# A matmul-bound retention, MLP and mixture-attention kernel: own PSUM banks for turned tiles, seven products for one more block, new ranks

## The chip, the cores and the metric

The kernel runs on one core of a Trainium2 chip. The metric is the device time of one launch in microseconds (us). The kernel before takes 442.72 us, the median of three runs (442.19 to 445.38). Lower is better.

## The reference

Three stages follow each other on 2 sequences of 768 tokens, all in float32.

```python
# 1. retention, 8 heads of 64, per head:  state = gamma*state + k_t v_t^T ;  y_t = q_t state / 8
# 2. MLP on x (768 x 512):
xn = (x - mu) / np.sqrt(var + 1e-06) * g_ln
ch = np.maximum(xn @ w_ch1, 0.0) @ w_ch2          # 512 -> 2048 -> 512
x = x + ch
# 3. mixture of 4 attention experts of width 64, the best 2 per token:
logits = x @ w_gate                                # top 2 of 4, softmax of the two -> w
q, k, v = x @ wq[e], x @ wk[e], x @ wv[e]
a = softmax(causal(q @ k.T / 8)); ye = a @ v @ wo[e]
out = sum over the two chosen experts of w * ye
```

## The kernel before, in words

**Front.** Retention is done in chunks of 128 tokens: 12 chunks (6 for each sequence b), each by `r_tile`. A chunk loads `kq` (512 KB) and `vk` (512 KB; 256 KB in each sequence's last chunk). TensorE computes scores (line 581), the part that comes from the state (600), the part inside the chunk (610) and the new state (618). VectorE scales into `xT`; TensorE turns that tile (`turn`, line 422) into PSUM, VectorE takes mean and variance from there (642), GpSimd the root (650), ScalarE normalises out of PSUM (`xn`, 655), TensorE turns it back (422) and ScalarE copies it to `xc` (664). The two turned tiles of a chunk are of kind `pb`. In the kernel before, a `pb` or `pc` tile is half of two PSUM banks, at the same columns of both (1024 words hold two such tiles), so two turned tiles share a pair of banks.

**MLP.** The 2048 hidden columns are worked in 8 blocks `f` of 256. Each float32 number is split into a rounded high part and the rest (`h`, `l`), and each product is three matmuls (high x high, high x low, low x high). Blocks 0 and 1 take plain products (`m_h`, line 766, then `m_c`, line 788). In blocks 2 to 7 (`SEVEN`) the first product, over both halves of the 768 tokens at once, goes by `m_h7` (line 858): seven half-sized products and sums of them (Strassen's scheme in Winograd's form) in place of eight. It needs sums of the weights (`w_sums`, GpSimd, in blocks 2 and 3 VectorE too) and of the tokens (`x_sums`). The second product, `m_c`, is plain in all blocks. The weights come as 64-bit floats and are cut down to 32 bits by ScalarE, GpSimd and VectorE (`split_piece`, lines 685 to 719).

**Attention.** `q_proj` (952) and `q_val` (976) make q, k and v of one sequence. `a_scores` works a strip of 128 queries against the keys before it for two experts: TensorE (1047), VectorE adds the mask and takes the row maximum (1054), ScalarE the exponential (1062), VectorE the inverse sum (1068, 1069), GpSimd scales the strip (1076). `a_turn` turns pieces of four 128-wide slots through PSUM (`pc` tiles, line 422) and ScalarE or VectorE copies each out (`COPY`, 446). `a_value` (1117) multiplies by v, `a_out` (1144) by `wo`, and the rows leave by DMA. The strips of two query chunks, for a pair of experts, are turned and multiplied together: 12 such groups in all.

**What sets the order.** Nothing is issued in the order of the code. Every step is a `Node` with a cost for each engine that may run it, and `Plan.issue` is a list scheduler: on each engine the ready step of lowest `prio` goes next, where `prio` is the place in the code plus a number from the table `RANK`, if its tiles find free places in SBUF and PSUM (`PL` lists the places of each kind). The instructions are then recorded in that order, and each engine's queue runs strictly in it. TensorE steps have a form (`whole`, `rows`, `columns`, `quarters`: the piece of the array that a matmul uses), and the planner charges `SWITCH` for each change of form. `spin` steps are idle matmuls at the start, before data arrive.

```python
    PL["pb"] = [("P", 1024 * i + 256 * k, 256) for i in (1, 2, 3) for k in range(2)]
    PL["pc"] = [("P", 1024 * i + 256 * k, 256) for i in (3, 2) for k in range(2)]
...
    def DMA(nbytes, fn, r=(), w=()):
        P.add({"D": nbytes / 372e3 + 0.03}, lambda e: fn(), r, w, lat=2.2)
```

Of the kernel before, what the change touches and what calls it, by code (L numbers as in the profile page):

```python
# [19 lines left out]
try:  # L20
# [27 lines left out]
ALONE = 4  # L48
SWITCH = 0.125
LAST = 10000  # L50
FILL = 12
TWO = ("pb", "pc")
# [6 lines left out]
WORDS = 205 * KB  # L59
QUEUES = {"ps1": "s", "ps2": "s", "pr": "pr", "pt": "pt", "ptn": "pt", "sm": "sm", "at": "at", "w": "w", "h": "h", "raw": "raw", "wy": "wy",  # L60
          "w1": "w1", "S": "S", "t": "t", "u": "u", "sf": "sf",
          "am": "am", "vs": "vs", "xn": "xn", "xc": "xc"}
ROUNDED = {"x", "w", "w1", "S", "t", "h", "wq", "wk", "wv", "wo", "qk0", "qk1", "at"}


class Buf:
# [1249 lines left out]
```

## Time and profile before

| | |
|---|---|
| median of 3 runs | 442.72 us (442.19 to 445.38) |
| the profiled execution | 442.45 us, its span 440.7 us, so 1.75 us lie around the span |
| TensorE (PE) busy | 429.4 us, 97% of the span |
| PE weight loads | 402.4 us, beside the matmuls |
| VectorE (DVE), ScalarE (ACT), GpSimd (POOL) busy | 309.8, 217.7, 212.0 us |
| chain that ended last | PE 90%, ACT 3%, DVE 2%, DMA 2%, POOL 1% |
| mean granted TensorE clock | 0.999 of full speed |

How to read it: an engine's queue runs in order, so a wait of one instruction holds all behind it. PE's busy time is not PE at its peak, since matmuls overlap; what a step takes of PE is the time from its start to the start of the next one. The chain of waits goes back from the last instruction, and here it stays on PE for nine tenths of the span.

### The profile page before, as it was taken

The page shows a single profiled execution, that of the slowest core. Times are in us where ns is not written, and L with a number is a line of the kernel's source. Part 1 is how long each engine was busy: PE and PEld are TensorE (multiplying, and loading weights), DVE is VectorE, ACT ScalarE, POOL GpSimd, SP SyncE. Part 2 cuts the span into 40 slices and gives each one's busy share as a digit, 9 for nine tenths or more (in the row PEclk, how much of TensorE's full clock was granted, in tenths as well). Part 3 has the DMA queues.
Part 4 walks back from the last instruction along what each step waited for, and adds up shares of the span by engine and source line. Part 5 has one row for each costly group of instructions (what it writes and reads, how often), then busy time and mean ns, then how long its engine had stood idle before and what let it go on. Part 6 is the DMA issues. An engine that isn't in the chain of part 4 may idle for free.

```text
span 440.7 us, 9076 instructions
## 1 busy us (share of the span) xinstructions
PE 429.4 (97%) x3546; PEld 402.4 (91%) x3546; DVE 309.8 (70%) x743; ACT 217.7 (49%) x460; POOL 212.0 (48%) x219
## 2 busy tenths in 40 slices
PE   9988999999999999999999999999999999999996
PEld 8877889999999999999999999999999877887765
DVE  2769978765778876868877655668556778667663
ACT  1568775342656346335353264234533666656552
POOL 2668865999999528117136054200401343422430
PEclk9999999999999999999999999999999999999999
DMA  8999432210322304104112002001100001001121
GB/s 288 328 337 345 133 109 84 97 49 1 106 86 92 101 0 143 50 1 136 54 59 88 1 1 96 1 0 55 48 1 1 1 12 39 2 0 49 50 97 49
DMA packets 11995, 35.18 MB, mean 80 GB/s; under 512 B 1840, under 2 KB 2480, under 8 KB 11952
## 3 DMA queue, kind: packets, MB, share of 16 engines
q1 hardware_dynamic: 11952, 34.60, 22.7%
q8 instruction: 28, 0.46, 0.4%
q14 instruction: 15, 0.12, 0.1%
HBM read 31.45 MB, written 3.15 MB: 79 GB/s over the span
## 4 chain that ended last, share of the span: by engine, by line
PE 90%; ACT 3%; DVE 2%; DMA 2%; POOL 1%; issue 1%; SPq 0%; POOLq 0%; DVEq 0%
PE ps L788 30%; PE ps L858 20%; PE ps L766 8%; PE ps L952 8%; PE ps L1117 4%; PE ps L976 4%; PE ps L422 4%; PE ps L1144 4%; PE ps L1047 3%; DMA raw<-in_w_dram 2%; PE ps L529 2%; PE ps L610 1%; PE ps L581 1%; ACT xn L655 1%; PE ps L600 1%
## 5 line engine op out<-in xcount | busy, mean ns | idle before, releaser
L788 PE MATMUL ps<-h,w 128*128 128x384 f32 x768 | 142.4, 335 | 0.0
L788 PEld LDWEIGHTS ps<-h,w 128*128 128x128 f32 x768 | 133.7, 188 | 0.7 <-DVE ps L798 0.3
L794 DVE TENSOR_TENSOR xT<-xT,ps 128x384 f32<-128x384 f32 x112 | 60.2, 550 | 30.6 <-PE ps L788 30.1
L1076 POOL TENSOR_SCALAR pr<-pr,sm,gate 128x384 f32<-128x384 f32 (+5 forms) x48 | 34.0, 718 | 77.9 <-DVE sm L1069 34.1
L719 POOL TENSOR_TENSOR w<-wy,w 128x512 fp32r<-128x512 f32 x26 | 34.0, 1319 | 38.1 <-PE ps L788 23.4
L858 PE MATMUL ps<-t,S 128*128 128x384 f32 x216 | 42.1, 334 | 0.0
L858 PEld LDWEIGHTS ps<-t,S 128*128 128x128 f32 x216 | 37.8, 188 | 0.0
L1062 ACT ACTIVATE pr<-pr,sm 128x384 f32<-128x384 f32 (+5 forms) x48 | 31.7, 663 | 9.9 <-DVE sm L1054 9.9
L766 PE MATMUL ps<-x,w 128*128 128x384 f32 x192 | 35.2, 337 | 0.0
L877 ACT ACTIVATE h<-ps 128x384 fp32r<-128x384 f32 x36 | 17.7, 490 | 32.9 <-PE ps L788 20.6
L766 PEld LDWEIGHTS ps<-x,w 128*128 128x128 f32 x192 | 33.2, 188 | 0.3
L685 ACT ACTIVATE wx<-raw 128x512 f32<-128x512 f32 x32 | 21.5, 671 | 23.8 <-DVE ps L692 16.0
L687 POOL TENSOR_SCALAR wx<-wx 128x512 f32<-128x512 f32 x32 | 20.0, 625 | 23.9 <-ACT wx L685 23.0
L867 ACT ACTIVATE u<-ps 128x384 f32<-128x384 f32 x36 | 17.5, 488 | 25.3 <-PE ps L858 16.6
L858 PE MATMUL ps<-x,w 128*128 128x384 f32 x144 | 28.6, 334 | 0.0
L689 DVE TENSOR_SCALAR ps<-wx 128x512 uint32<-128x512 uint32 x32 | 22.0, 688 | 6.4 <-POOL wx L687 6.1
L858 PEld LDWEIGHTS ps<-x,w 128*128 128x128 f32 x144 | 25.3, 188 | 0.0
L1054 DVE CUSTOM_DVE_ANT_0 pr<-ps,mask 128x384 f32<-128x384 f32 (+4 forms) x48 | 22.1, 495 | 3.2 <-PE ps L1047 2.2
L695 DVE SCALAR_TENSOR_TENSOR wy<-raw,ps 128x512 uint32<-128x512 uint32 x32 | 21.8, 683 | 2.3 <-POOL w L719 1.7
L879 DVE SCALAR_TENSOR_TENSOR h<-ps,h 128x384 fp32r<-128x384 f32 x36 | 19.4, 551 | 5.3 <-ACT h L877 5.2
L692 DVE SCALAR_TENSOR_TENSOR ps<-wx,ps 128x512 uint32<-128x512 uint32 x32 | 22.2, 695 | 1.1
L587 DVE TENSOR_TENSOR am<-ps,caus 128x512 f32<-128x512 f32 x24 | 15.5, 683 | 9.9 <-PE ps L581 9.9
(122 smaller groups left out, 822.7 us busy)
## 6 DMA issues: line engine op xcount, KB each, us to landing
raw<-in_w_dram SPq DMA_DIRECT2D x32, 512.0 KB, 3.4
kq<-in_kq_dram SPq DMA_DIRECT2D x11, 512.0 KB, 5.1
vk<-in_vk_dram SPq DMA_DIRECT2D x9, 512.0 KB, 5.5
out_dram<-ob SPq DMA_DIRECT2D x11, 256.0 KB, 2.0
vk<-in_vk_dram SPq DMA_DIRECT2D x4, 256.0 KB, 3.8
vraw<-in_wv_dram SPq DMA_DIRECT2D x1, 520.0 KB, 3.9
kq<-in_kq_dram SPq DMA_DIRECT2D x2, 256.0 KB, 5.2
mraw<-in_wk_dram SPq DMA_DIRECT2D x1, 512.0 KB, 4.6
```

What stands on the lines that cost most here:

```text
L689: DVE(0.69, lambda: dve.tensor_scalar(u32(z), u32(x), 4, 1, op0=OP.logical_shift_left, op1=OP.logical_shift_right), r=[x], w=[z])
L692: DVE(0.7, lambda: dve.scalar_tensor_tensor(u32(z), u32(x), 0x80000000, u32(z), op0=OP.bitwise_and, op1=OP.bitwise_or), r=[x, z], w=[z])
L695: DVE(0.7, lambda: dve.scalar_tensor_tensor(u32(y), words(0), 29, u32(z), op0=OP.logical_shift_right, op1=OP.bitwise_or), r=[raw, z], w=[y])
L719: POOL(1.3, lambda: pool.tensor_tensor(f32r(l), f32(y), f32(h), OP.subtract), r=[y, h], w=[l])
L766: pe.matmul(f32(pa, TB), lhsT=wt, rhs=blk(f32r(xt[b][j]))[:, k], start=(n == 0), stop=(n == 11))
L788: pe.matmul(f32(pa, TB), lhsT=wt, rhs=t, start=(n == 0), stop=(n == 5))
L794: DVE(0.55, lambda: dve.tensor_tensor(blk(f32(xt))[:, k], blk(f32(xt))[:, k], f32(pa, TB), OP.add), r=[pa] + [(xt, cc, w) for cc in range( ...
L858: pe.matmul(f32(pa, TB), lhsT=wt, rhs=t, start=(first and n == 0), stop=(n == 5), skip_group_check=True)
L952: pe.matmul(f32(pa, TB), lhsT=mw(n, lo, k, p * 128, (p + 1) * 128), rhs=blk(f32r(xt))[:, k], start=(i == 0), stop=(i == 11))
L1054: DVE(0.22 + wide * 1.04e-3, lambda ks=ks, n=n, z=z, SC=SC: dve.tensor_tensor_reduce(f32(PR[z])[:, ks], f32(SC[z])[:, :wide], f32(MASK)[:, ...
L1062: ACT(act_c(nk) + .18, lambda pr=pr, z=z: act.activation(f32(pr, nk), f32(pr, nk), AF.Exp, bias=f32(sm)[:, z:z + 1], scale=-1.0, accum_out ...
L1076: POOL(0.34 + nk * 0.84e-3, lambda pr=pr, z=z, e=e: pool.tensor_scalar(f32(pr, nk), f32(pr, nk), f32(sm)[:, 6 + z:7 + z], GT[b, j][:, cc, ...
```

## The change

- A turned tile (`pb`, `pc`) gets two whole PSUM banks of its own; `pb` has three places in place of six, `pc` four in place of four halves. Scores (`ps1`) and attention outputs (`psa`) may lie in all eight banks. `a_turn` cuts its slots into two equal pieces rather than pieces of four (40 pieces in place of 48).
- In the last block, f = 7 (`BOTH`), the second product goes by seven products too: `m_c7`, seven products of three matmuls for each half r of the output columns, with sums of the hidden values (`ht`, made by GpSimd) and of the second weights (`S2`). `leave` is the old end of `m_c`.
- The quarter sum `c22` of `m_h7` stays in PSUM rather than in SBUF.
- `kq` and `vk` get more places (6 and 4 for 4 and 3), as do other tiles; `WORDS` grows, and the DMA scratch area is set to 1024.
- The planner's costs change: a DMA at 335 KB/us in place of 372, lead times of the engines (`LEAD`), `w_sums` on GpSimd alone. The state is one key in place of two. All of `RANK` is new, so the order is new on every engine.

```diff
@@ -46,21 +46,22 @@
+BOTH = (7,)
 SWITCH = 0.125
+LEAD = {"V": 0.085, "A": 0.1, "G": 0.05}
...
 RANK = {
-    "a_out 1": (16, (46, 145, 47, 97, -108, 150, -14, -17)),
+    "a_out 1": (16, (-6, 10, -14, 15, 85, 136, -22, 123)),
...
-        n.eng = eng
+        n.eng = {e: c - LEAD.get(e, 0.0) for e, c in eng.items()}
         n.fn = fn
-        n.lat = lat
+        n.lat = lat + max(LEAD.get(e, 0.0) for e in eng)
...
+    PL["kq"] += region(o_z, 4 * KB, 2)
+    PL["vk"] += region(o_z + 8 * KB, 4 * KB, 1)
...
-    PL["psa"] = banks[4:][::-1]
-    PL["ps1"] = banks[:4]
+    PL["psa"] = banks[::-1]
+    PL["ps1"] = banks
     PL["state"] = banks[:1]
 
-    PL["pb"] = [("P", 1024 * i + 256 * k, 256) for i in (1, 2, 3) for k in range(2)]
-    PL["pc"] = [("P", 1024 * i + 256 * k, 256) for i in (3, 2) for k in range(2)]
-
-    def two(b):
-        i, k = divmod(b.at[1], 1024)
-        return ps[:, 1024 * i:1024 * i + 1024].rearrange("p (h c) -> p h c", h=2)[:, :, k:k + 256]
+    PL["pb"] = [("P", 1024 * i, 1024) for i in (1, 2, 3)]
+    PL["pc"] = [("P", 1024 * i, 1024) for i in (3, 2, 1, 0)]
+
+    def two(b, n=256):
+        return view(b).rearrange("p (h c) -> p h c", h=2)[:, :, :n]
...
     def DMA(nbytes, fn, r=(), w=()):
-        P.add({"D": nbytes / 372e3 + 0.03}, lambda e: fn(), r, w, lat=2.2)
+        P.add({"D": nbytes / 335e3 + 0.03}, lambda e: fn(), r, w, lat=2.2)
...
         W[f, i] = (h, l)
+        if f in BOTH and i >= 2:
+            W[f, i + 2] = y
+            if i == 3:
+                w_sums(f, W[f, 4], y, True)
...
+        def out(src, n):
+            h = l = None
+            if f in BOTH:
+                t = HT[n]
+                P.at = "m_h7 4"
+                ACT(0.49, lambda: act.activation(plain(t), f32(src, TB), AF.Relu), r=[src], w=[t])
+                if n == 2:
+                    return
+                h, l = new("h"), new("h")
+                P.at = "m_h7 5"
+                ACT(0.42, lambda: act.activation(f32r(h, TB), plain(t), AF.Copy), r=[t], w=[h])
...
-        c22 = new("u")
+        c22 = new("ps")
         add(c22, pc, u3)
...
+        if f in BOTH:
+            ht = [new("ht") for _ in range(4)]
+            for t, p, q in ((0, 2, 0), (2, 1, 2), (1, 1, 0), (3, 3, 1)):
+                P.at = "m_h7 8"
+                POOL(0.93, lambda t=t, p=p, q=q: pool.tensor_tensor(plain(HT[t]), plain(HT[p]), plain(HT[q]), OP.subtract),
+                     r=[HT[p], HT[q]], w=[HT[t]])
+            for t in range(4):
+                P.at = "m_h7 9"
+                ACT(0.42, lambda t=t: act.activation(f32r(ht[t]), plain(HT[t]), AF.Copy), r=[HT[t]], w=[ht[t]])
+                P.at = "m_h7 10"
+                POOL(0.93, lambda t=t: pool.tensor_tensor(f32r(HT[t]), plain(HT[t]), f32(ht[t]), OP.subtract), r=[HT[t], ht[t]], w=[HT[t]])
+            return m_c7(f, b, {"x00": h00, "x10": h10, "x11": h11, **{f"t{t}": (ht[t], HT[t]) for t in range(4)}})
         return [h00, h10], [h01, h11]
+
+    def m_c7(f, b, tokens):
+        def second(r):
+            pa, pb, pc = (new("ps") for _ in range(3))
...
+                def mm():
+                    for i, (wt, t) in enumerate(((wh, xh), (wh, xl), (wl, xh))):
+                        pe.matmul(f32(pa, TB), lhsT=f32r(wt)[:, cs], rhs=f32r(t, TB), start=(first and i == 0), stop=(i == 2),
+                                  skip_group_check=True)
...
+            product(pa, "a0", "x00", True)
+            c1 = keep(pa)
+            yield
+            product(pb, "s1", "t1", True)
+            add(pb, pb, c1)
+            yield
+            product(pa, "y0", "x10", False)
+            leave(pa, b, 0, r)
...
-            dve.tensor_scalar(m[:, 4:6], m[:, 2:4], 1e-9, None, op0=OP.add)
+            for z in range(2):
+                dve.tensor_scalar(m[:, 4 + z:5 + z], m[:, 2 + z:3 + z], 1e-9, None, op0=OP.add)
...
-            for s0 in range(0, len(slots), 4):
-                part = slots[s0:s0 + 4]
+            half = (len(slots) + 1) // 2 if len(slots) > 4 else len(slots)
+            for s0 in range(0, len(slots), half):
+                part = slots[s0:s0 + half]
```

Three places of the new order follow, each before and after. In names like `kq_90` the number tells tiles of one kind apart; it differs between the two kernels.

TensorE at the very start of the program; `negs` rows are the idle matmuls, `kq` rows the scores of a chunk. Before:

```order
L529 MATMUL ps<-negs 128x128 x14
L581 MATMUL ps<-kq_90 128x128 x8
L581 MATMUL ps<-kq_85 128x128 x8
L529 MATMUL ps<-negs 128x128 x2
L610 MATMUL ps<-am_124,vs_109 64x128 x4
L610 MATMUL ps<-am_128,vs_109 64x128 x4
```

After:

```order
L546 MATMUL ps<-negs 128x128 x10
L598 MATMUL ps<-kq_83 128x128 x8
L546 MATMUL ps<-negs 128x128 x3
L627 MATMUL ps<-am_111,vs_107 64x128 x4
L627 MATMUL ps<-am_116,vs_107 64x128 x4
L546 MATMUL ps<-negs 128x128
```

The first chunk's scores stand behind 10 idle matmuls rather than 14, one chunk's scores go first rather than two, and four of the idle matmuls moved behind them (six in all there, for two).

SyncE's queue of loads, in the middle of the front; `raw` rows are pieces of MLP weights, `kq` and `vk` the chunks' data. Before:

```order
L505 DMA vk_322<-in_vk_dram 128x1024
L495 DMA kq_361<-in_kq_dram 128x1024
L678 DMA raw_377<-in_w_dram 128x1024
L505 DMA vk_404<-in_vk_dram 128x1024
L678 DMA raw_444<-in_w_dram 128x1024
L495 DMA kq_469<-in_kq_dram 128x1024
```

After:

```order
L522 DMA vk_443<-in_vk_dram 128x1024
L522 DMA vk_470<-in_vk_dram 128x1024
L512 DMA kq_504<-in_kq_dram 128x1024
L695 DMA raw_532<-in_w_dram 128x1024
L695 DMA raw_558<-in_w_dram 128x1024
L512 DMA kq_595<-in_kq_dram 128x1024
```

The first piece of weights is the 27th load of the queue rather than the 22nd, and the second stands right behind it: more of the chunks' data go ahead of the weights.

TensorE in the last MLP block. Before, the last rows of its plain second product, with scores of the attention already between them:

```order
L788 MATMUL ps<-h_3483,w_3049 128x384
L788 MATMUL ps<-h_3487,w_3051 128x384
L788 MATMUL ps<-h_3497,w_3051 128x384
L788 MATMUL ps<-h_3487,w_3067 128x384
L1047 MATMUL ps<-qk_531_3896,qk_547_4030 128x384 x2
L1047 MATMUL ps<-qk_531_3896,qk_548_4048 128x384 x2
```

After, where the first product with a sum of hidden values begins (`ht` and `S`; sequence b = 0); the `L811` rows ahead of it are the plain second product of block 6:

```order
L811 MATMUL ps<-h_3184,w_2757 128x384
L811 MATMUL ps<-h_3194,w_2757 128x384
L811 MATMUL ps<-h_3184,w_2771 128x384
L978 MATMUL ps<-ht_3340,S_426_2989 128x384
L978 MATMUL ps<-ht_3353,S_426_2989 128x384
L978 MATMUL ps<-ht_3340,S_428_3000 128x384
```

The last block's second product is now 84 matmuls (`L978`) in place of 96, spread among the rest of block 6, the first product of b = 1 and the first projections. 44 matmuls of other steps stand between the last matmul of `m_h7` of b = 0 and the first `ht` row, and 39 for b = 1. The first scores of the attention stand at row 1,693 of PE's order, where they stood at row 1,577.

## Rows read from the trace of the kernel before

**Rows 1.** Busy time by stage (windows): us, PE, PEld, DVE, ACT, POOL.

```profile
12.00:50.50 38.50, 34.60 (x691) 29.58 (x689) 30.66 (x75) 26.48 (x57) 28.49 (x38) 1.00 0.86 305
82.70:319.00 236.30, 236.30 (x1363) 235.87 (x1362) 169.67 (x305) 105.76 (x200) 124.00 (x101) 1.00 0.17 57
319.00:437.00 118.00, 115.21 (x1113) 96.66 (x1112) 79.18 (x301) 63.22 (x166) 33.99 (x48) 1.00 0.07 25
```

**Rows 2.** Who PE waited for: us in total, times, longest.

```profile
PE ps L422 <- DVE pt L446: 1.6, 3, 0.7
PE ps L422 <- ACT xn L655: 1.2, 1, 1.2
...
PE ps L422 <- ACT ptn L446: 0.7, 2, 0.4
```

**Rows 3.** PE in the MLP, in order of time: start, us, what.

```profile
82.70 8.49 PE L788 MATMUL ps<-h,w 128*128 128x384 f32 x48
91.03 8.48 PE L766 MATMUL ps<-x,w 128*128 128x384 f32 x48
```

**Rows 4.** PE where the form changes, in order of time.

```profile
24.08 0.41 PE L422 MATMUL ps<-ident,xn 64*128 64x64 f32 x8
24.33 0.42 PE L422 MATMUL ps<-ident,xT 64*128 64x64 f32 x8
24.68 0.67 PE L600 MATMUL ps<-kq,sn 64*64 64x128 f32 x16
...
50.50 2.38 PE L766 MATMUL ps<-x,w 128*128 128x384 f32 x12
52.81 0.46 PE L422 MATMUL ps<-ident,xn 64*128 64x64 f32 x8
53.20 2.37 PE L766 MATMUL ps<-x,w 128*128 128x384 f32 x12
```

**Rows 5.** PE at the start, in order of time.

```profile
1.05 6.00 PE L529 MATMUL ps<-negs 128*128 128x128 f32 x28 [1.05 <-DVE half L546]
6.98 2.08 PE L581 MATMUL ps<-kq 64*128 64x128 f32 x32
```

**Rows 6.** ACT in the front and PE behind it, in order of time, all engines.

```profile
28.10 0.67 ACT L685 ACTIVATE wx<-raw 128x512 f32<-128x512 f32 x1 [1.10 <-DMA raw<-in_w_dram]
...
28.94 0.77 ACT L655 ACTIVATE xn<-ps,mv 128x512 f32<-128x512 f32 x1
...
29.76 0.46 PE L422 MATMUL ps<-ident,xT 64*128 64x64 f32 x8 [1.20 <-ACT xn L655]
```

**Rows 7.** Two turned tiles in one pair of banks, in order of time.

```profile
15.90 0.78 ACT L655 ACTIVATE xn<-ps,mv 128x512 f32<-128x512 f32 x1 [1.47 <-issue]
16.71 0.76 DVE L642 BATCH_NORM_STATS2 mv<-ps 128x6 f32<-128x256 f32 x2 [0.57 <-ACT xn L655]
```

**Rows 8.** From the last scores to their first turn, all engines, in order of time.

```profile
420.68 1.29 PE L1047 MATMUL ps<-qk,qk 64*128 64x384 f32 x12
...
424.43 0.62 DVE L1054 CUSTOM_DVE_ANT_0 pr<-ps,mask,sm 128x384 f32<-128x384 f32 x1
...
427.55 1.95 POOL L1076 TENSOR_SCALAR pr<-pr,sm,gate 128x768 f32<-128x768 f32 x2 [2.10 <-DVE sm L1069]
428.65 0.77 PE L422 MATMUL ps<-ident,pr 64*128 64x64 f32 x17
```

**Rows 9.** Groups by line and shape: busy, mean ns of one, idle before.

```profile
L719 POOL TENSOR_TENSOR w<-wy,w 128x512 fp32r<-128x512 f32 x26 | 34.0, 1319 | 38.1 <-PE ps L788 23.4 <-ACT w L717 14.7
L710 POOL TENSOR_TENSOR w<-wy,w 128x256 fp32r<-128x256 f32 x6 | 4.5, 744 | 6.3 <-ACT w L707 4.7 <-PE ps L858 1.6
```

**Rows 10.** The same view for ScalarE.

```profile
L877 ACT ACTIVATE h<-ps 128x384 fp32r<-128x384 f32 x36 | 17.7, 490 | 32.9 <-PE ps L788 20.6 <-PE ps L858 9.5 <-DVE ps L872 2.7
```

**Rows 11.** The same view for VectorE.

```profile
L872 DVE TENSOR_TENSOR ps<-ps,u 128x384 f32<-128x384 f32 x24 | 13.6, 565 | 8.9 <-PE ps L858 8.3 <-ACT x L801 0.5
...
L1068 DVE TENSOR_SCALAR sm<-sm 128x2 f32<-128x2 f32 x24 | 4.0, 168 | 4.1 <-ACT pr L1062 4.0
```

More of the change, by code (lines that the diff above doesn't have):

```diff
@@ L218, in fits @@
                 for o in live.get(sp, ()):
-                    if (o.users or o.end > t) and any(x < y + size and y < x + o.at[2] for x in strips(o.kind, o.at[1])
-                                                      for y in strips(b.kind, off)):
+                    if (o.users or o.end > t) and o.at[1] < off + size and off < o.at[1] + o.at[2]:
                         break
@@ L739, in w_sums @@
         P.at = "w_sums 3"
-        P.add({"V": 2.4, "G": 2.41} if f < ALONE else {"G": 2.5}, lambda e: (dve if e == "V" else pool).tensor_tensor(f32r(l), f32(t), f32(h), OP.subtract),
+        P.add({"G": 2.5}, lambda e: (dve if e == "V" else pool).tensor_tensor(f32r(l), f32(t), f32(h), OP.subtract),
               r=[h] + [(t, i) for i in range(4)], w=[l])
-        W[f, "S"] = (h, l)
-        P.writer["sums"] = P.nodes[-1]
+        W[f, "S2" if second else "S"] = (h, l)
+        if not second:
+            P.writer["sums"] = P.nodes[-1]
     def w1_at(f, k, m):
@@ L872, in add @@
             DVE(0.55, lambda: dve.tensor_tensor(f32(dst, TB), f32(pa, TB), f32(u), OP.add), r=[pa, u], w=[dst])
-        def out(src):
-            h, l = new("h"), new("h")
-            P.at = "m_h7 4"
-            ACT(0.49, lambda: act.activation(f32r(h, TB), f32(src, TB), AF.Relu), r=[src], w=[h])
-            P.at = "m_h7 5"
+        def out(src, n):
[9 more added lines that the diff above has]
+                ACT(0.42, lambda: act.activation(f32r(h, TB), plain(t), AF.Copy), r=[t], w=[h])
+            else:
+                h, l = new("h"), new("h")
+                P.at = "m_h7 6"
+                ACT(0.49, lambda: act.activation(f32r(h, TB), f32(src, TB), AF.Relu), r=[src], w=[h])
+            P.at = "m_h7 7"
             DVE(0.55, lambda: dve.scalar_tensor_tensor(f32r(l, TB), f32(src, TB), 0.0, f32(h, TB), op0=OP.max,
@@ L881, in out @@
             return h, l
+        HT = [new("ht") for _ in range(4)] if f in BOTH else None
         pa, pb, pc = (new("ps") for _ in range(3))
         def go_on(n=1):
-            for _ in range(min(n, len(rest))):
-                m_c(*rest.pop(0))
+            for _ in range(min(n * (2 if len(rest) > 8 else 1), len(rest))):
+                go(rest.pop(0))
         product(pa, "a11", "x00", True)
@@ L893, in m_h7 @@
         product(pa, "y0", "x10", False)
-        h00 = out(pa)
+        h00 = out(pa, 0)
         u2 = keep(pb)
@@ L904, in m_h7 @@
         product(pb, "y1", "t3", False)
-        h10 = out(pb)
+        h10 = out(pb, 3)
         go_on()
@@ new lines, in m_h7, with product, keep, add @@
+        return [h00, h10], [h01, h11]
+    def m_c7(f, b, tokens):
+        def second(r):
+            pa, pb, pc = (new("ps") for _ in range(3))
+            def product(pa, wn, xn, first):
+                (wh, wl), c0 = ((W[f, 2 + (wn[0] == "y")], 256 * int(wn[1])) if wn[0] in "ay" else (W[f, "S2"], 256 * int(wn[1])))
+                xh, xl = tokens[xn]
+                cs = slice(c0 + 128 * r, c0 + 128 * r + 128)
+                def mm():
+                    for i, (wt, t) in enumerate(((wh, xh), (wh, xl), (wl, xh))):
+                        pe.matmul(f32(pa, TB), lhsT=f32r(wt)[:, cs], rhs=f32r(t, TB), start=(first and i == 0), stop=(i == 2),
+                                  skip_group_check=True)
+                P.at = "m_c7 1"
+                PE(0.52, mm, r=[wh, wl, xh, xl], w=[pa])
+            def keep(pa):
+                u = new("u2")
+                P.at = "m_c7 2"
+                ACT(0.49, lambda: act.activation(f32(u), f32(pa, TB), AF.Copy), r=[pa], w=[u])
+                return u
+            def add(dst, pa, u):
+                P.at = "m_c7 3"
+                DVE(0.55, lambda: dve.tensor_tensor(f32(dst, TB), f32(pa, TB), f32(u), OP.add), r=[pa, u], w=[dst])
+            product(pa, "a0", "x00", True)
[6 more added lines that the diff above has]
+            leave(pa, b, 0, r)
+            u2 = keep(pb)
+            yield
+            product(pc, "s0", "t0", True)
+            yield
+            product(pb, "s2", "t2", False)
+            u3 = keep(pb)
+            c22 = new("ps")
+            add(c22, pc, u3)
+            yield
+            product(pb, "y1", "t3", False)
+            leave(pb, b, 0, 2 + r)
+            yield
+            product(pc, "s3", "x11", False)
+            add(pc, pc, u2)
+            leave(pc, b, 1, r)
+            leave(c22, b, 1, 2 + r)
+            yield
+        one, two = second(0), second(1)
+        return [one, two] * 7 if b == B - 1 else [one] * 7 + [two] * 7
@@ L1105, in a_value @@
         nj = 2 * g + 2
+        half = (0, 4, 6)[g]
+        needs = {j0: sorted({min((2 * j0 + i) // half, 1) if half else 0 for i in (0, 3)}) for j0 in range(0, nj, 2)}
         avs, at = [new("psa") for _ in range(2 if last else 1)], new("at")
@@ L1122, in a_value @@
                 PE((0.87 if j0 + 2 < nj else 0.65) * len(zs) / 2, mm, form="columns",
-                   r=[VV[b, j0], VV[b, j0 + 1]] + [(pt, j0 // 2) for pt in (*PT, *also)], w=[av])
+                   r=[VV[b, j0], VV[b, j0 + 1]] + [(pt, i) for pt in (*PT, *also) for i in needs[j0]], w=[av])
             cs = slice(zs[0] * C, (zs[-1] + 1) * C)
@@ L1190, in flush @@
         while rest:
-            m_c(*rest.pop(0))
+            go(rest.pop(0))
     for n, (f, b, j) in enumerate(steps):
@@ L1212, in retention_channel_mlp_mixture_attention @@
             flush()
-            rest = [(f, b, jj, hh, k) for jj, hh in enumerate(hs) for k in range(NK)]
+            rest = hs if f in BOTH else [(f, b, jj, hh, k) for jj, hh in enumerate(hs) for k in range(NK)]
     load_mw("wv")
```

77 lines of the change are left out of this document (42 added, 35 removed), and 151 rows, old and new, of the table RANK.

## The prediction

> **What bounds the kernel now.** I read the page first: TensorE (PE) is busy for 97% of the span and the chain of waits lies on PE for 90%. So I ask how much PE work the change takes away, and what becomes of the time in which PE waits.
>
> The windows show three stages [rows 1]. From 12 to 50.5 us, the front, PE is idle for 38.5 - 34.6 = 3.9 us. From 82.7 to 319 us, the MLP, it is never idle. From 319 to 437 us, projections and attention, it is idle for 118.0 - 115.2 = 2.8 us. These 6.7 us are all that better waits can give back; the rest is PE's own work.
>
> The list of waits names them [rows 2]: in the front a turn that waits for ACT's `xn`, in the attention turns that wait until earlier turned tiles are copied out of PSUM (1.6 and 0.7 us in the rows shown). Two places show why. In the front ACT stands 1.10 us behind the first piece of weights, and `xn`, queued behind it, comes late for PE by 1.20 us [rows 6]. And VectorE's statistics of one turned tile start at 16.71, 0.03 us after ACT's `xn` of another ends (15.90 + 0.78 = 16.68), having waited 0.57 us for it though they read different tiles in one pair of banks [rows 7].
>
> **The change, term by term.** The sum is made against the profiled execution's own 442.45 us; the median of the runs is 0.27 us higher.
>
> *Matmuls.* The last block's second product takes 84 in place of 96. In the MLP 48 matmuls take 91.03 - 82.70 = 8.33 us, so 0.1735 each [rows 3]. They stand on PE, which does not wait there: -12 x 0.1735 = **-2.1 us**.
>
> *Form changes.* Counted in PE's order, changes from the whole array to a part of it fall from 29 to 21, those back from 29 to 21, and those between parts rise from 43 to 47. Twelve matmuls before a turn take 52.81 - 50.50 = 2.31 us where 12 x 0.1735 = 2.08 stand: 0.23 for the way in. Eight turns take 53.20 - 52.81 = 0.39 before a matmul and 24.33 - 24.08 = 0.25 before other turns: 0.14 for the way back. Before a quarter form they take 24.68 - 24.33 = 0.35: 0.10 between parts [rows 4]. That is -8 x 0.23 - 8 x 0.14 + 4 x 0.10 = -2.6; since some changes fall where PE waits anyway, and some between parts cost less, I take **-2.2 us** (bounds -2.6 and -1.5).
>
> *Start.* 14 idle matmuls take 6.98 - 1.05 = 5.93 us, 0.42 each, and hold the first scores though these need only one load [rows 5]. With four fewer ahead the first scores may start 1.7 us earlier, if the data are there: ahead of the first half of `kq` now lie 64 KB, where 768 KB lay before. Four idle matmuls and two more form changes (counted above) stand behind them instead, where PE waits for masks and scaled values at least in part. Between -1.7 and 0 I take **-0.8 us**.
>
> *Front waits.* 3.9 us now. The first piece of weights is now the 27th load, not the 22nd, so ACT should not stand before it as in rows 6 (-1.2 us), and statistics and `xn` of two tiles no longer share banks. Against it: each turned tile holds two banks alone, and there are three places for six. Bounds: -3.9 (no wait) and +6.8 (worked out under B). I take **-1.2 us**, 2.7 us left, since one of the causes is shown and removed and the other resource is not seen to run out here.
>
> *Attention waits.* 2.8 us now. What a group of strips needs is the chain from its last scores to its first turn: the scores end at 420.68 + 1.29 = 421.97, VectorE, ACT, VectorE and GpSimd follow, and the turn begins at 428.65: 6.7 us [rows 8]. PE needs other work of that length between them. Pricing the steps between them with rows like rows 3 and 4, four of the 12 groups had less before (5.5, 5.5, 6.0 and 6.3 us: 3.5 us short in all, against 2.8 us of idle time); now five have less (4.6, 5.2, 5.3, 5.4 and 5.8 us). Of these, 4.6 and 5.2 belong to strips of at most 256 keys, whose chain is shorter. The other three are 3.6 us short, as much as before. The change adds one small VectorE instruction to the chain, 0.17 us [rows 11]. Waits on copies of shared banks go, worth up to the 2.3 us of rows 2. Bounds -2.5 and +11; I take **+0.4 us**.
>
> *The new chain in the last block.* PE's last product of `m_h7` is followed by an add (0.57), ACT's ReLU (0.49) and GpSimd subtractions [rows 10, 11]. For one of 128 x 384 I take the middle of 0.74 and 1.32 us, 1.03 [rows 9]. For b = 0 the first product with sums needs six of them: with some 0.4 us of passing on, 0.57 + 0.49 + 0.4 + 6 x 1.03 = 7.6 us, and 44 matmuls, 7.6 us, cover it. For b = 1 it needs five: 6.6 us under 39 matmuls, 6.8 us. The cover is exact, so a short wait is likely: **+0.2 us** (0 to +3, the latter if a subtraction takes the full 1.32 us). VectorE's and ACT's other additions in the MLP cost nothing: VectorE is busy there for 170 of 236 us, ACT for 106, and PE never waits for them [rows 1]. `c22` in PSUM likewise.
>
> Sum: -2.1 - 2.2 - 0.8 - 1.2 + 0.4 + 0.2 = -5.7, so **436.8 us**.
>
> **The rivals.**
>
> *B, the front runs short of PSUM.* Turned tiles need twice the banks, so a turn waits until an earlier tile has been read through. For: the six banks also hold scores and sums. Against: the new order leaves 3.9 us or more of PE work between a tile's first turn and its second, about the chain between them. The only price in the trace is the 0.57 us of rows 7. Once for each of 12 chunks it is 6.8 us on top, 443.6; for every second chunk 440.2. The Trainium skill, page "TensorEngine Tiling (Array Packing)", section "Gotcha 1: PSUM Pressure", speaks against the change in the same way: row tiles must write to different banks, so row tiling costs banks. The trace agrees as far as it goes: the turns work on 64 rows [rows 4].
>
> *C, the waits go.* If ACT's stand and all waits for copies out of shared banks go, 1 us is left in the front and 0.8 in the attention: 436.8 - 1.7 - 2.4 = 432.7. For: the named waits of rows 2 are of these kinds. Against: a turn can wait for the copy of its own places too. The Trainium skill, page "PSUM — Partial Sum Buffer", section "PSUM bank collisions raise a hardware error", says that two engines may not touch one bank at a time, readers included, and that software has to keep them apart. The trace agrees (0.03 us between the two reads in rows 7). By that rule alone every wait between two turned tiles goes with the sharing, and the time is C's.
>
> *S, slower: the attention runs short of cover.* Its place is the five groups named above. Work that could fill PE between scores and turns is used up earlier, since the first scores come later in PE's order. If the chain takes 7.0 us in each group rather than 6.7, the five are 8.7 us short, 442.3, as slow as before: that is the point from which it decides. At 7.5 us they are 11.2 us short: 436.8 - 3.2 + 11.2 = 444.8. For: the added VectorE instruction makes it 6.9. Against: the chain of rows 8 holds queueing (GpSimd starts 2.5 us after VectorE's last mask), and two of the five groups are short strips.
>
> That the matmuls saved do not show would take PE waits in the MLP, where there are none now; the chain of the last block is the one place for it, at most 3 us, inside the range.
>
> **Numbers.** My forecast, from 434.5 to 440, has a chance of 0.56, B 0.17, C 0.17, S 0.10. The predicted time is the forecast's. The range goes from 432.5 to 443: it leaves out C's lower end, B's upper end and most of S. About 1%, 4.4 us, is what a measurement of this kernel can tell from no change: faster means below 438.3, slower above 447.1. Faster are all of C and some 0.40 of the forecast's 0.56: 0.57. Slower is only S with a chain near 8 us: 0.04. The same: 0.39.
>
> **What would show it.** In the profile after: 0.173 us from matmul to matmul and 84 of them in the last block's second product; first scores between 5.3 and 6.5 us; the first MLP matmul near 49 us; no wait of ACT for `raw` that a turn inherits; no VectorE statistics that wait for another tile's `xn`; about 3 us of PE idle time in the front and as much in the attention. Idle time in the front above 6 us, before turns, means B; below 1.5 us in both stages, C; idle time of 8 us and more in the attention, before turns and behind GpSimd, S. An idle PE in the MLP, before the first product with `ht`, would show my costs of GpSimd wrong. I am wrong altogether if PE's own steps got longer.

## The result and the profile after

The changed kernel takes 437.60 us, the median of four runs (435.65 to 441.59), against 442.74 for the kernel before beside it: a ratio of 0.9899, 95% interval 0.9864 to 0.9934. Six more runs of the same kernel (e1 below) gave a median of 436.22, ratio 0.9859 (0.9826 to 0.9893). The forecast was 436.8.

The ten runs lie within 6.5 us; the first four of the kernel before lie within 3.2, 22 later ones within 4.5. The execution first profiled took the longest, 441.59 us with a span of 439.8. It shows where the spread lies, and it has to be read beside a common one. First its windows; the columns are those of [rows 1], the granted clock behind the busy times of the five engines:

```profile
5.50:13.40 7.90, 5.30 (x69) 4.40 (x70) 2.14 (x4) 0.38 (x1) 1.04 (x1) 0.92 0.96 335
13.40:20.00 6.60, 6.60 (x88) 5.87 (x84) 4.03 (x9) 1.16 (x2) 2.87 (x4) 0.58 0.71 263
20.00:41.40 21.40, 19.29 (x404) 17.01 (x403) 16.00 (x42) 15.38 (x36) 14.78 (x19) 1.00 0.88 323
41.40:50.00 8.60, 7.85 (x106) 6.43 (x108) 6.44 (x13) 7.14 (x15) 6.56 (x10) 0.60 0.71 273
...
89.40:315.00 225.60, 225.53 (x1295) 224.12 (x1295) 156.31 (x289) 108.19 (x211) 137.87 (x122) 1.00 0.17 57
315.00:436.00 121.00, 120.94 (x1167) 106.23 (x1167) 87.65 (x340) 68.42 (x172) 39.98 (x52) 1.00 0.07 25
```

Two things stand out against [rows 1]. In the attention PE is idle for 0.06 us, where it was idle for 2.8. And in the front the granted clock falls twice, to 0.50 (1.2 of 2.4 GHz) from 12.12 to 18.95 us and from 42.84 to 49.67; the means of these two windows are 0.58 and 0.60. What came before each fall stands in the list of what PE waited for, the same execution:

```profile
PE ps L439 <- ACT xc L681: 1.9, 1, 1.9
PE ps L439 <- DMA ident<-in_ident_dram: 1.7, 1, 1.7
...
PE ps L617 <- ACT xc L681: 0.7, 1, 0.7
PE ps L635 <- DMA vk<-in_vk_dram: 0.7, 1, 0.7
```

In order of time (SPq is the DMA queue's own row), the same execution:

```profile
6.72 0.33 SPq L512 DMA_DIRECT2D kq<-in_kq_dram  x1
7.09 0.43 SPq L557 DMA_DIRECT2D ident<-in_ident_dram  x1
...
12.96 0.69 PE L439 MATMUL ps<-ident,xT 64*128 64x64 f32 x8 [1.68 <-DMA ident<-in_ident_dram]
13.41 3.75 PE L598 MATMUL ps<-kq 64*128 64x128 f32 x32
...
40.14 0.66 ACT L702 ACTIVATE wx<-raw 128x512 f32<-128x512 f32 x1 [2.03 <-DMA raw<-in_w_dram]
40.71 0.58 ACT L681 ACTIVATE xc<-ps 128x512 f32<-128x512 f32 x1
...
41.34 0.46 PE L439 MATMUL ps<-ident,xT 64*128 64x64 f32 x8 [1.92 <-ACT xc L681]
```

The 64 KB of `ident` are issued only behind a `kq` that waits at 6.72 us, so the first turn comes 1.68 us late; the 32 scores behind it take 3.75 us where 2.06 to 2.08 is their time at full clock ([rows 5] and the execution of e10 below). At 40 us ACT stands 2.03 us for the first piece of weights, with the `xc` copy that PE wants behind it. The prediction had that stand gone [rows 6]; it is there again, 0.9 us longer, and a turn inherits it.

A common execution is that of e1, 435.87 us, span 434.0:

```profile
5.23:12.00 6.77, 5.02 (x61) 3.94 (x60) 2.04 (x4) 0.38 (x1) 1.04 (x1) 0.97 0.85 310
12.00:51.17 39.17, 37.16 (x720) 32.50 (x720) 31.88 (x77) 27.78 (x60) 29.19 (x38) 0.96 0.87 314
...
304.80:429.30 124.50, 124.39 (x1184) 109.39 (x1184) 89.09 (x343) 71.95 (x179) 44.19 (x56) 1.00 0.07 23
```

Here PE is idle for 1.75 us between the first scores and 12 us, for 2.0 in the rest of the front (3.9 before), for 0.1 in the attention. The first MLP matmul starts at 51.17 us (57.06 in the execution first profiled). It was to be near 49, and in the kernel before it starts at 50.50. The new chain in the last block shows in both as two short stands, before the first product with sums of each sequence (the execution first profiled; six matmuls without a stand have a row of 1.20 us, three of 0.68):

```profile
292.17 1.20 PE L811 MATMUL ps<-h,w 128*128 128x384 f32 x6
293.21 1.49 PE L978 MATMUL ps<-ht,S 128*128 128x384 f32 x6
...
312.24 1.02 PE L978 MATMUL ps<-ht,S 128*128 128x384 f32 x3
313.10 0.68 PE L978 MATMUL ps<-h,w 128*128 128x384 f32 x3
```

They are 0.29 and 0.34 us. The prediction took such a stand for a sign of wrong costs of GpSimd, but the costs were right. GpSimd's subtractions take 1.016 us each, where 1.03 had been taken from between the two sizes of [rows 9] (groups by line and shape, the same execution):

```profile
L957 POOL TENSOR_TENSOR ht<-ht,ht 128x384 f32<-128x384 f32 x8 | 8.1, 1016 | 7.1 <-ACT ht L907 6.6
```

### The profile page after: what moved, and what is told of

Same layout as the page of the kernel before. It is cut to its first block, busy times and chain, and to the rows that moved or that the text cites. A ratio compares the mean times of both kernels' runs of the same rounds, so it can differ in the third digit from the quotient of the medians.

```text
span 439.8 us, 9139 instructions
## 1 busy us (share of the span) xinstructions
PE 429.3 (98%) x3534; PEld 404.4 (92%) x3534; DVE 308.6 (70%) x770; ACT 228.6 (52%) x485; POOL 233.9 (53%) x244
## 4 chain that ended last, share of the span: by engine, by line
PE 89%; DMA 3%; ACT 2%; POOL 2%; DVE 2%; issue 1%; SPq 0%; POOLq 0%; ACTq 0%
PE ps L811 25%; PE ps L886 19%; PE ps L789 8%; PE ps L1059 8%; PE ps L1228 4%; PE ps L1255 4%; PE ps L1154 4%; PE ps L439 4%; PE ps L1083 4%; PE ps L978 2%; DMA raw<-in_w_dram 2%; PE ps L598 2%; PE ps L627 2%; DMA ident<-in_ident_dram 1%; PE ps L617 1%; PE ps L546 1%
## 5 line engine op out<-in xcount | busy, mean ns | idle before, releaser
L811 PE MATMUL ps<-h,w 128*128 128x384 f32 x672 | 126.1, 334 | 0.0
L811 PEld LDWEIGHTS ps<-h,w 128*128 128x128 f32 x672 | 117.2, 188 | 0.4 <-DVE xT L817 0.3
L918 DVE SCALAR_TENSOR_TENSOR h<-ps,h 128x384 fp32r<-128x384 f32 x46 | 24.9, 551 | 9.7 <-ACT h L916 4.9
L900 DVE TENSOR_TENSOR ps<-ps,u 128x384 f32<-128x384 f32 x36 | 20.2, 562 | 12.5 <-ACT u L895 7.1
L916 ACT ACTIVATE h<-ps 128x384 fp32r<-128x384 f32 x40 | 19.0, 486 | 17.2 <-PE ps L811 9.7
L734 ACT ACTIVATE w<-wy 128x512 fp32r<-128x512 f32 x26 | 16.1, 628 | 19.3 <-PE ps L811 19.0
```

The source lines that it names most:

```text
L811: pe.matmul(f32(pa, TB), lhsT=wt, rhs=t, start=(n == 0), stop=(n == 5))
L918: DVE(0.55, lambda: dve.scalar_tensor_tensor(f32r(l, TB), f32(src, TB), 0.0, f32(h, TB), op0=OP.max, op1=OP.subtract), r=[src, h], w=[l])
```

## The experiments

Several of them keep every engine's order as the planner made it and move one load, one step or the place of a tile in the finished list. Where the planner runs again instead, the text says so. "Before" is the kernel before, timed beside each of them; its medians are 441.84 to 442.74 us, so times of different experiments can be compared to about 0.9 us.

### e1: the changed kernel again

No edit.

> The changed kernel once more, unaltered. Theory T: its runs differ because loads land at different times. In the profiled execution PE stood 1.7 us for the load of ident and 1.9 us for an xc that stood behind the first piece of weights, and after each the granted clock was 0.5 for 4 to 6 us. Where both land in time the run takes about 435.5, where both are late 441.6; the median stays between 436.5 and 439, and the profile of this run shows a clock share that goes with its time. Rival R: the spread is the chip's and not the loads'; then times and waits for loads do not go together.

436.22 us (435.05 to 438.39). The profiled run, 435.87 us, waited 0.2 us for `ident`, and ACT stood 0.3 us for weights. The clock shares of the runs go with their times at the ends: 435.05 and 435.47 had 1.000, 438.39 had 0.990, and of the first four 441.59 had 0.983 and 435.65 had 1.000. In between (0.996 at 435.87, 436.56 and 437.70) they do not order the runs. More can be read from the traces. In e1, e4, e5, e9 and e12 every engine's order is that of the execution first profiled up to 236 us at least, so there are six profiled executions of one front. Its first MLP matmul starts at 57.06 us in the first, and at 51.17, 50.43, 51.80, 51.11 and 53.15 in these five; the clock falls twice in the first, once in e1, e9 and e12, and in e4 and e5 not at all. So this front alone spreads by 6.6 us. The slowest execution has T's two waits and the falls behind them; but e4 and e5 lie 1.4 us apart at full clock, and which waits for loads the runs without a profile had is not known. T holds for the slow end, and for the middle R is not excluded.

### e2, e3: loads and one step of ScalarE moved

```diff
 # e2, in the finished order
+        k = next(i for i, (n, e) in enumerate(order) if n.at[0] == "ident")
+        loads = [i for i, (n, e) in enumerate(order[:k]) if e == "D"]
+        order.insert(loads[-1], order.pop(k))
 # e3, on top: the first split step behind the next xc copy
+        k = next(i for i, (n, e) in enumerate(order) if n.at == ("split_piece 1", 0))
+        x = next(i for i, (n, e) in enumerate(order) if i > k and n.at[0] == "r_tile 14")
...
+        order.insert(x, order.pop(k))
```

> The changed kernel, with the load of ident one place earlier in SyncE's queue, ahead of the third kq, which waits until PE has read the first scores out of the place it reuses; every other queue as it is. T: ident is issued at 4.5 us, not 7.1, the first turn no longer waits 1.7 us, and the fall of the clock behind it (4.6 us at half speed) does not come; the slow runs go and the median falls by 1 to 3 us against e1. R: the median stays within 0.7 us of e1.

> As e2, and ScalarE's first step on a piece of weights stands behind the xc copy that it stood ahead of; nothing else moves. T: the 1.9 us that PE waited for that xc go in every run, and the clock's fall at 42 us with them; median 434.5 to 436, all runs within 2 us. R: as e2 within 0.7 us, since weights that come later are waited for elsewhere.

e2: 435.43 us (434.33 to 435.80), ratio 0.9828 (0.9803 to 0.9853). `ident` was issued at 4.47 us and nothing waited for it. The median is 0.8 us below e1, less than T had and just more than R, and the intervals overlap; what changed is that none of six runs is above 435.8, where five of the ten runs of the changed kernel are above 436.8. PE still waits 1.55 us for the second half of the first `vk`, and the clock still falls behind that. Nor is `ident` all of it: e3, which has it early too, has a run of 438.21 us at a clock share of 0.991.

e3: 436.30 us (435.37 to 438.21), ratio 0.9855 (0.9827 to 0.9883). T failed: the median is above 436, the runs lie within 2.8 us, and in the profiles of e1 and e2 ACT hardly stood for the weights, so there was little to win. In e3's own profile ACT stood 1.1 us for the weights again, now behind the `xc`, and PE waited 0.9 us for the `xn` that comes after: the stand had only moved to the next step in ACT's queue. That is R's reason; the median is 0.9 us above e2, a little more than R's 0.7, and the intervals overlap.

### e10, e11: the first loads

```diff
 # e10, on e2: the second kq behind the second half of vk and ident
+        q = next(i for i, (n, e) in enumerate(order) if n.at == ("load 1", 3))
+        k = next(i for i, (n, e) in enumerate(order) if n.at[0] == "ident")
+        order.insert(k, order.pop(q))
 # e11, on e10: the kq that PE takes first is loaded first, into the first place that is free over its life
+        k = next(i for i, (n, e) in enumerate(order) if n.at == ("load 1", 2))
+        q = next(i for i, (n, e) in enumerate(order) if n.at == ("load 1", 3))
...
+        order.insert(q, order.pop(k))
...
+                b.at = p
```

> As e2, and the second kq is loaded behind the second half of vk and ident rather than ahead of them. T (the front's early loads set the rest): PE's wait of 1.55 us for vk at 9 us goes, the clock does not fall behind it, and the median is 0.8 to 2 us below e2; rival: the second kq then comes late for the 32 scores at 13 us, and it is within 0.5 us of e2 or slower.

> As e10, and the kq that PE takes first at 12 us is loaded first of the two and into a free place, so that its load no longer waits for PE to finish the first scores (issued at 4.5 us, not 6.0). T: it lands some 1.5 us earlier, PE's wait of 1.54 us for it falls below 0.5, and the median is 0.7 to 1.5 us below e10. Rival: the loads are already at the rate that the queue can give from 4 us on, so another load comes late in its place, and it is within 0.5 us of e10.

e10: 435.20 us (434.64 to 436.30), ratio 0.9835 (0.9805 to 0.9866). The wait for `vk` went, and a wait of 1.54 us for `kq` took its place, three steps later (e10, then e11, PE in order of time):

```profile
10.16 0.46 PE L446 MATMUL ps<-ident,xT 64*128 64x64 f32 x8
...
12.16 2.06 PE L605 MATMUL ps<-kq 64*128 64x128 f32 x32 [1.54 <-DMA kq<-in_kq_dram]
```

```profile
10.89 0.46 PE L462 MATMUL ps<-ident,xT 64*128 64x64 f32 x8
11.19 2.01 PE L621 MATMUL ps<-kq 64*128 64x128 f32 x32
```

e11: 435.19 us (433.91 to 435.58), ratio 0.9829 (0.9807 to 0.9850). That wait went too, the first scores came at 5.62 us rather than 4.85, and PE waits 0.80 us for another `kq` at 34 us. The rivals were right in both: the DMA engines are busy for 0.89 to 1.06 of the time in each 2 us from 4 to 16 us in e10, so moving one load ahead makes another late. Of these kernels e2, e10 and e11 have the lowest medians; they cannot be told apart, nor from e1 by the intervals.

### e4, e5: the plain second product in the last block

```diff
-BOTH = (7,)
+BOTH = ()
 # e5 only, in m_c
-        if True:
+        if f == NFC - 1:
+            leave(pa, b, j, k)
+        else:
```

> The changed kernel with a plain second product in the last block too (12 matmuls more, no sums of hidden values). If the seven products save what they take out of PE: 12 x 0.1735 = 2.1 us, less 0.2 to 0.6 us of waits for the new chain, so 1.5 to 1.9 us slower than e1. Rival: the new order around it was made for the seven products and the plain one loses more, 3 us and up, in the waits of the attention; or the saving is given back, and it is within 0.5 us of e1.

> The changed kernel with a plain second product in the last block, its sums leaving for the attention as before. As e4, with that step in place. If the seven products are worth what they take out of PE, it is 1.5 to 2.1 us slower than e1 (12 matmuls of 0.1735 us more, two short waits for sums of hidden values less). Rival: the projections then wait for the last product's way out, 3 us and up; or they gain nothing, within 0.5 us.

In e4 the way out of the last block is gone with the seven products, so that its attention reads the MLP's input and waits for nothing of the MLP: 438.15 us. e5 has the way out: 438.32 us (437.27 to 440.39), ratio 0.9903 (0.9867 to 0.9939), 2.1 us above e1's median. The planner ran again, but every engine's order is that of e1 up to 236 us, and PE's idle time in the attention is as short as in e1 (0.12 us of 123.7). From step to step the MLP takes 1.6 us more than in e1 (255.8 against 254.2), which is about the 2.1 us of 12 matmuls less the two stands; most of the rest between these two executions is in the front, whose order is the same. The seven products are worth about what they take out of PE, less the stands. The intervals of e5 and e1 overlap, so by the medians alone the size is known to no better than some 2 us.

### e8: the same order with shared banks

In the finished order of e2, 10 turned tiles of the attention and 4 of the front are put into the pair of banks that another turned tile holds at that time, beside it, where the pair is otherwise free.

```diff
+                if (o is not b and o.kind == b.kind and o not in taken and b not in taken and life[o][0] <= life[b][0] <= life[o][1]
...
+                    b.at = ("P", 1024 * i + 256, 768)
...
-        return view(b).rearrange("p (h c) -> p h c", h=2)[:, :, :n]
+        i, k = divmod(b.at[1], 1024)
+        return ps[:, 1024 * i:1024 * i + 1024].rearrange("p (h c) -> p h c", h=2)[:, :, k:k + n]
```

> As e2 (the changed kernel with ident earlier), every engine's order the same, but 10 of the attention's turned tiles and 4 of the front's put into the pair of banks that another holds, as it was before. K: the waits of one reader for the other are back, 0.3 to 0.7 us each, and the time rises by 1 to 4 us against e2. N: the readers wait, but PE has other work; within 0.5 us of e2.

439.70 us (439.00 to 441.13), ratio 0.9936 (0.9916 to 0.9955): 4.3 us above e2, a little more than K's most, and the intervals are apart. No instruction stands elsewhere. The first MLP matmul starts at 51.19 us against 51.17, so all of the difference is in the attention. What the four tiles of the front cost is not shown by that: in the front the clock fell in e2 and not in e8, PE is 1.3 us ahead in e8 at 17 us and level again at 39. The attention (e2, then e8, the window from the same matmul to the end):

```profile
304.80:429.30 124.50, 124.37 (x1185) 109.44 (x1184) 89.16 (x343) 72.07 (x179) 44.30 (x56) 1.00 0.07 24
```

```profile
304.80:433.50 128.70, 125.43 (x1185) 109.61 (x1185) 89.95 (x343) 72.08 (x179) 44.58 (x57) 1.00 0.06 23
```

Idle time of PE rises from 0.13 to 3.27 us. One place shows how. In e2 PE turns four tiles into four pairs (6, 8, 6 and 8 of the 28 matmuls), ACT copies the first out from 358.67 while PE is still turning the others, DVE copies the second from 358.91 on, and PE goes on with scores at 359.21:

```profile
358.22 1.12 PE L442 MATMUL ps<-ident,pr 64*128 64x64 f32 x28
...
358.67 0.93 ACT L466 ACTIVATE ptn<-ps 128x384 f32<-128x384 f32 x2 [1.27 <-PE ps L442]
...
358.91 1.29 DVE L466 COPY ptn<-ps 128x512 f32<-128x512 f32 x2
359.21 1.32 PE L1157 MATMUL ps<-qk,qk 64*128 64x384 f32 x12
```

In e8 the first two lie in one pair, and the last two in another. ACT starts only when PE has turned both of the first pair, DVE only when ACT has read, and PE's scores wait for DVE. These are waits for semaphores, which the program sets: in e8 PE's signal to ACT comes with the 14th matmul, in e2 with the sixth.

```profile
358.89 1.09 PE L461 MATMUL ps<-ident,pr 64*128 64x64 f32 x28
...
359.57 0.94 ACT L485 ACTIVATE ptn<-ps 128x384 f32<-128x384 f32 x2 [1.52 <-PE ps L461]
360.10 1.29 DVE L485 COPY ptn<-ps 128x512 f32<-128x512 f32 x2 [0.61 <-ACT ptn L485]
360.84 1.04 PE L1176 MATMUL ps<-qk,qk 64*128 64x384 f32 x8 [0.87 <-DVE ptn L485]
```

From the turn to the scores it is 0.99 us with own banks and 1.95 us with shared ones. The Trainium skill, page "PSUM — Partial Sum Buffer", section "PSUM bank collisions raise a hardware error", has two engines' accesses to one bank kept apart whichever columns they touch; the three engines standing in a row here agree with it (ACT's read ends at 360.07, and DVE's read of the other tile of the pair starts at 360.10).

### e7: own banks in the old order

In the finished order of the kernel before, 15 of the 29 turned tiles of the attention that share a pair with another tile are moved to a pair that is free for their whole life.

```diff
+        for b in sorted((b for b in life if b.kind in ('pc',)), key=lambda b: life[b][0]):
+            if used(b.at[1] // 1024, b):
...
+                for i in (3, 2, 1, 0):
+                    if not used(i, b):
+                        b.at = ("P", 1024 * i, 256)
...
+                        break
```

> The kernel before, every engine's order as it was, but 15 of the attention's turned tiles moved from a shared pair of PSUM banks to a free pair (29 share one with another tile; for the other 14 no pair is free or their partner has gone). Theory K: PE's idle 2.8 us in the attention came from reads of shared banks keeping each other waiting; then it falls to 1 to 1.8 us and the time by 1 to 1.8. Rival N: it came from the order, which left too little work between scores and turns; then the idle time stays within 0.5 us and so does the time.

444.85 us (443.45 to 448.03), ratio 1.0054 (1.0029 to 1.0079): slower, which neither theory had. PE's idle time in the attention did not fall: it is 3.6 us, against 2.8. PE and ACT at one of the moved tiles:

```profile
344.59 0.64 PE L439 MATMUL ps<-ident,pr 64*128 64x64 f32 x13 [0.23 <-DVE qk L979]
...
345.09 0.98 ACT L463 ACTIVATE ptn<-ps 128x512 f32<-128x512 f32 x2 [1.14 <-PE ps L439]
...
345.74 0.65 PE L439 MATMUL ps<-ident,pr 64*128 64x64 f32 x14 [0.50 <-ACT ptn L463]
```

The old order turns four pieces behind one another, into four halves of two pairs. Two tiles alone in two pairs leave the third piece no place until ACT has copied the first, and PE stands 0.50 us there; in the trace of before it goes through. So a bank of its own is a gain for the readers and a loss of places, and the order decides which is larger.

### e9, e12, e13: parts undone or done alone, with the planner run again

```diff
 # e9: the ranks of before for the steps of attention and projections
-    "a_out 1": (16, (-6, 10, -14, 15, 85, 136, -22, 123)),
+    'a_out 1': (16, (46, 145, 47, 97, -108, 150, -14, -17)),
 ...
 # e12: pieces of four slots
-            half = (len(slots) + 1) // 2 if len(slots) > 4 else len(slots)
+            half = 4
 # e13, in the kernel before
-    PL["pb"] = [("P", 1024 * i + 256 * k, 256) for i in (1, 2, 3) for k in range(2)]
-    PL["pc"] = [("P", 1024 * i + 256 * k, 256) for i in (3, 2) for k in range(2)]
+    PL["pb"] = [("P", 1024 * i, 1024) for i in (1, 2, 3)]
+    PL["pc"] = [("P", 1024 * i, 1024) for i in (3, 2, 1, 0)]
```

> The changed kernel with the ranks of the kernel before for every step of the attention and its projections (a step without one there has none); all else, own banks included, as in e1. Theory K: own banks take the attention's waits away whatever the ranks; PE idle in the attention stays below 1 us and the time within 1 us of e1. Rival N: the new ranks gave PE its cover; idle time of 2 us and more is back, and the time is 2 to 8 us above e1.

> The changed kernel with the attention's turned pieces cut at four slots again (48 pieces, not 40), in banks of their own. If the fewer pieces saved form changes: 8 of them, each 0.23 into the turn and 0.14 out where a piece stood alone, 1.5 to 2.6 us slower than e1. Rival: pieces of one group stand one behind the other anyway, and it is within 0.7 us of e1.

> The kernel before with two banks of its own for every turned tile (three places in the front, four in the attention, and scores and outputs of the attention in all eight banks), its old ranks and all else. K: the attention's idle 2.8 us fall to below 1 us; the front, at three places, is no slower than 1 us; the time is 1 to 3 us below before. N: ranks that were made for shared banks don't fit, and it is within 1 us of before or slower.

All three are slower than the kernel before: e9 452.98 us (ratio 1.0235, 1.0206 to 1.0264), e12 444.93 (1.0066, 1.0041 to 1.0091), e13 470.45 (1.0642, 1.0610 to 1.0674). e9 answers its question: with own banks and old ranks PE waits again, 8.3 us idle in the attention, and its clock falls (list of waits from 312 us on, then two windows):

```profile
PE ps L438 <- POOL pr L1183: 6.7, 3, 2.8
```

```profile
400.00:402.50 2.50, 0.71 (x8) 0.52 (x8) 0.69 (x5) 0.81 (x4) 2.05 (x5) 0.50 0.00 0
402.50:406.00 3.50, 3.50 (x34) 2.58 (x32) 2.23 (x5) 1.57 (x4) 0.79 (x2) 0.50 0.02 5
```

So the banks alone do not take the waits away: N was right that the order gives the cover, though e9 is 16.8 us above e1, twice N's most, and e8 had shown that the banks matter in the order that was made for them.

e12 and e13 do not answer their questions. e12's order is that of e1 on every engine up to 370 us, and what it loses lies behind that: from step to step its attention takes 7.9 us more than in e1, with PE idle for 3.5 us (2.2 of them for GpSimd's strips), a granted clock of 0.50 from 401.5 to 404.9 us, and 26 changes from the whole array to a part of it and 26 back, where e1 has 21 of each. At the prices of the prediction these changes are worth some 2 us (an estimate: 5 x 0.23 + 5 x 0.14, and two more between parts at 0.10). What pieces of four cost by themselves stays open. In e13 the order is another one from 15 us on, and 13 us of PE idle time are in the stretch from 46 to 330 us, the MLP, which the edit does not touch: so it prices ranks that were set for other places more than the banks.

## Why the prediction was right, and where it was not

The total was right because two parts of it were wrong in opposite directions; that they cancel is luck. Summed from the start of each step to the start of the next, by the kind of matmul, e1 takes 6.7 us less than the kernel before: 118.3 against 124.4 in the attention and its projections (-6.1; the very last step, which has no next, is left out), 254.2 against 255.6 in the MLP (-1.4), and 0.8 more in the front with its idle matmuls. By the terms of the prediction these should have been -1.8, -1.9 and -2.0. The attention is the same within 0.1 us in all six profiled executions that have its new order and places (the first, e1, e2, e3, e10, e11); the front takes 0.4 us less to 6.7 more than before in them.

- **Matmuls, -2.1.** Right: the rows stand 0.173 us apart in the last block as elsewhere, and the MLP of e5 is 1.6 us longer, which with the two stands makes 2.2.
- **New chain, +0.2.** Right in kind, 0.6 us in two stands; the durations taken for it were right (1.016 us for 1.03).
- **Form changes, -2.2.** Too small, if anything: of the attention's 6.1 us, 2.7 are idle time of PE, and the other 3.4 lie in the changes of form and between the steps. No experiment shows them alone; e12 was to, and does not.
- **Attention waits, +0.4.** The step that failed: 2.8 us became 0.1. I had set the chain of [rows 8], 6.7 us, as what each group needs and counted five groups short of it. They were not short: PE stood at none of them, so what was needed was no more than the 4.6 to 5.8 us that they had. The 6.7 us held queueing, part of it behind copies that stood behind other copies in shared banks, as reads do in [rows 7]. The rows below show it for the last group, first in the kernel before, then in e1: from the end of the last scores to the end of the reciprocal it is 5.41 us (421.97 to 427.38) and then 4.00 (412.35 to 416.35). In the kernel before VectorE has stood 0.62 us for ScalarE's copy of the neighbouring tile and is still copying when these scores end. I subtracted the waits on shared banks once, as PE's own waits, and left the chain at its old length. e8 gives the size in the new order: with 10 tiles of the attention back in shared pairs it is 4.3 us slower.

```profile
421.74 0.69 DVE L446 COPY pt<-ps 128x512 f32<-128x512 f32 x1 [0.62 <-ACT pt L446]
...
427.21 0.17 DVE L1069 RECIPROCAL sm<-sm 128x2 f32<-128x2 f32 x1
```

```profile
410.98 1.37 PE L1154 MATMUL ps<-qk,qk 64*128 64x384 f32 x12
...
416.18 0.17 DVE L1177 RECIPROCAL sm<-sm 128x2 f32<-128x2 f32 x1
```

- **Start, -0.8.** Wrong: nothing. The first scores start at 5.23 us rather than 6.98, and PE is then idle for 1.75 us, where it was not idle before. The first turn is at 12.09 us, against 12.18, and PE has done fewer products by then (the scores of one chunk for those of two). e10 and e11 show why: the loads fill the DMA engines, and what PE does earlier waits for data later.
- **Front waits, -1.2.** Wrong: in e1's idle time better, 3.9 to 2.0 us, but the clock is 0.62 of full speed there from 11.0 to 13.4 us and 0.69 from 13.4 to 16.0, and the first MLP matmul comes 0.7 us later than before, not earlier. The clock is not all of it. In e5, at full clock, the first MLP matmul starts at 51.80 us, and e8, at full clock, gets no further than e2: both turn at 45.6 us, after the same wait of 0.57 us for ACT's `xc`. What holds the front there is not shown. The first piece of weights is the 27th load, but by the trace of the kernel before it was the 23rd there and not the 22nd. No VectorE statistics wait for another tile's `xn` any more, as was foretold; what that is worth in time no run shows. Rival B's price shows in part: turns and products with the state wait for `xc` three times in e1, 1.6 us in all, where it was 1.1 before.

The rivals: C was half right, in the attention, and its front did not come. S did not come, but e9 shows that it is a real danger: with other ranks turns wait 6.7 us for GpSimd. Its price per group was of the right kind; the ranks, which I could read only as an order, kept it away.

What no step held is the spread. I took PE's waits at their length. In the execution first profiled two waits of 1.7 and 1.9 us cost PE more than that, since the clock fell behind each. From the 32 scores at 13.41 us to the start of the second chunk's intra-chunk products at 19.02 it is 5.6 us there, 4.2 in e1, whose clock fell less, and 3.1 in e10 at full clock (12.16 to 15.30). Around the second fall, from 41.34 to 49.10 us, the same steps take 2.4 us more than in e1. So 1.4 + 2.4 = 3.8 of the 5.8 us between the spans of these two executions are clock, and the rest is idle time. Executions in which the clock falls once or not at all differ for other reasons too (e1).

## What to carry to other kernels

Tiles that two engines read from one pair of banks make a chain out of copies that could run side by side; when you give them own banks, shorten that chain in your estimate too, and count the places that are lost: undoing it for 10 tiles cost 4.3 us in the order made for it, and doing it for 15 cost 2.4 in the order made without it. In a kernel whose order comes from tuned ranks, undo a part in the finished order where that can be done: planned again, e9, e12 and e13 came out 9 to 29 us slower than the kernel they were made from, and only e9 says something about its part. A small load that everything needs, such as `ident`, goes ahead of any load that waits for a place; and where loads fill the DMA engines, as here, starting earlier may gain nothing.

## What was not expected of the hardware

The clock's fall can be worth more than the wait behind which it comes. From the 32 scores to the second chunk's intra-chunk products it is 5.6 us in the execution first profiled, against 3.1 at full clock in e10: 2.5 us, behind a wait of 1.68. And waits of nearly the same length differ in it. In e2 PE ran an idle matmul, was idle for 1.55 us from 9.2 us on, and went on with products for the new state; the granted clock was 0.50 from 11.0 to 13.4 us. In e10 PE ran products for the new state, two idle matmuls and a turn, was idle for 1.54 us from 10.6 us on, and went on with scores; the granted clock stayed at 1.00. What decides between them these runs don't show.
